# Batch 0's decay rows issued by SP instead of GpSimd, and pair 1's K transposed one tile earlier with half of its copy on ScalarE

## The chip, the cores and the metric

The kernel runs on one core of a Trainium2 chip. The metric is the device time of one execution in microseconds; the time before is the median of three runs. The core's engines are named as in the profile: PE (TensorE), DVE (VectorE), ACT (ScalarE), POOL (GpSimd) and SP (SyncE). SP and POOL also issue the DMAs.

## The reference

Forgetting attention, followed by a small MLP. Shapes: 8 batches, 8 heads, 576 positions, head dimension 64; the MLP takes 4608 tokens of width 512 to 2048 and back.

```python
scores = scale * np.matmul(q, k.transpose(0, 1, 3, 2))
cum = np.cumsum(np.log(np.clip(f, 0.0001, 1.0)), axis=-1)
scores = np.where(causal, -1e9, scores + cum[..., :, None] - cum[..., None, :])
attn = softmax(scores);  x = (attn @ v) laid out as tokens x 512
h = x @ w_in;  out = (h - np.tanh(h)) @ w_out
```

The softmax is a plain one over the last axis. Results are float32.

## The kernel before

**Tiling.** The work of attention goes by pairs of heads: 8 batches x 4 pairs = 32 pairs, called p = 0 to 31 here. For a pair the kernel needs `QT` and `KT`, Q and K turned so that the head dimension lies on the partitions (64 rows), and three more rows under them that carry the decay: the scores' matmul runs over 67 rows, so that `cum[i] - cum[j]` comes out of the same product. The rows are two fp16 parts of the cumulated logarithm (`chi`, `clo`, L189 and L190) and constants (from `ones16` and `minus16`).

`scores` (L337) makes the seven tiles of a pair (`TILES`, L332: three for head 0, a small "tail" tile, index 3, with the last 64 positions of both heads, and three for head 1). In batch 0 the causal mask is added by another matmul with `late` (L355). Each tile ends in an exponential on ACT (L361, target `e`, or `el` for the tail tile). `values` (L382) multiplies by V, DVE divides (L398 to L400), `turn` (L407) puts the result into `XR`, and the MLP (`mlp1` L441, `mlp2_plain` L486, `mlp2` L506) follows in chunks of 512 tokens.

**Transposing Q and K.** `trans` (L287) transposes a pair's Q or K with six matmuls into a PSUM tile `t` (L298) and copies it out in two halves, even and odd positions. The string `copies` says who makes each half: "VV" is twice DVE (L311), "AV" is ACT (L309) for the first and DVE for the second. The two halves interleave in the same rows of `QT` or `KT`.

**Order.** Each engine's order is the order in which the program emits (a manual schedule). `start` (L570) makes pair 0's Q and K and its tiles 0 and 1; `bulk` (L209) issues the rest of batch 0's loads; then `att_items` (L591) lists, for each pair p and tile index `ti`, the scores, the transposes for the next pair (`at_q` and `at_k` say at which tile), the loads of `LOADS`, and `unread(n)` (L563): n matmuls of 128 columns on constants that nobody reads. In pair 0, `unread` stands after tiles 2, 5 and 6. Their PSUM tile `idle` has the bank "tr", which in batch 0 the tail tile of pair 0 and tile 0 of pair 1 use as well (L338, L339). The tiles 4, 5 and 6 use the two banks "sc".

**DMAs.** POOL issues all loads of q, k, v and the weights; they share its software queue (q0 in the profile). A software DMA waits for the one eight places earlier to have ended. SP issues the constant rows (`const_rows`, L202), the decay rows of batch 1 and later (`load_aug`, L198), the DMA transposes and the stores, on its own hardware queue (q1). Before, the three decay rows of batch 0 (seven heads each; head 0 has its rows from ACT at L572 and DVE at L191) go out from POOL at L211 to L213:

```python
(k_hi, chi_0), (k_lo, clo_0), (q_hi, _) = aug_rows(0)
nc.gpsimd.dma_start(out=k_hi, in_=chi_0)
nc.gpsimd.dma_start(out=q_hi, in_=chi_0)
nc.gpsimd.dma_start(out=k_lo, in_=clo_0)
```

The first work that reads these rows is the second head of pair 0's tail tile: head 1 is the first head whose rows come by DMA.

Of the kernel before, what the change touches and what calls it, by code (L numbers as in the profile page):

```python
# [21 lines left out]
def kernel(  # L22
# [10 lines left out]
    nc = tc.nc  # L33
# [7 lines left out]
    NPAIR = H // 2  # L41
# [51 lines left out]
    qn, kn = ([t[0:S // NT6, :].rearrange("p (h n d) -> p h n d", h=H, n=NT6) for t in raw] for raw in (qraw, kraw))  # L93
# [3 lines left out]
    KT = [qkp.tile([D + 3, H, PITCH], FP16, tag=f"KT{i}", name=f"KT{i}") for i in range(2)]  # L97
# [3 lines left out]
    def load_qk(dst, src, b, h0, h1):  # L101
        nc.gpsimd.dma_start(  # L102
            out=dst[b % 2][:, h0:h1, :, :].rearrange("p h n d -> p h (n d)"),
            in_=src[b, h0:h1, :, :].rearrange("h (p n) d -> p h (n d)", n=NT6))
# [25 lines left out]
    def load_v_block(b, n, h0, h1):  # L130
        nc.gpsimd.dma_start(out=vn[b % 2][:, n, h0:h1, 0:D],  # L131
                            in_=v[b, h0:h1, n * P:(n + 1) * P, :].rearrange("h p d -> p h d"))
# [60 lines left out]
    def aug_rows(b):  # L193
        i, h0 = b % 2, 0 if b else 1
        hs = slice(b * H + h0, (b + 1) * H)
        return [(KT[i][D:D + 1, h0:H, 0:S], chi[hs, :]), (KT[i][D + 1:D + 2, h0:H, 0:S], clo[hs, :]), (QT[i][D + 2:D + 3, h0:H, :], chi[hs, :])]

    def load_aug(b):  # L198
        for to, of in aug_rows(b):
            nc.sync.dma_start(out=to, in_=of)  # L200

    def const_rows(i):  # L202
        h0 = 1 - i
        nc.sync.dma_start(out=QT[i][D:D + 2, h0:H, :], in_=minus16[0:2 * (H - h0), :])
        nc.sync.dma_start(out=KT[i][D + 2:D + 3, h0:H, 0:S], in_=ones16[0:H - h0, :])
# [2 lines left out]

    def bulk():  # L209
        (k_hi, chi_0), (k_lo, clo_0), (q_hi, _) = aug_rows(0)  # L210
        nc.gpsimd.dma_start(out=k_hi, in_=chi_0)  # L211
        nc.gpsimd.dma_start(out=q_hi, in_=chi_0)
        nc.gpsimd.dma_start(out=k_lo, in_=clo_0)  # L213
        load_qk(qn, q, 0, 4, 6)
        load_qk(kn, k, 0, 4, 6)
        load_qk(qn, q, 0, 6, H)
        load_qk(kn, k, 0, 6, H)
        for n in range(NJ - 1):
            load_v_block(0, n, 2, H)
# [22 lines left out]
    for b in range(2, B):  # L242
        p0 = (b - 1) * NPAIR
        at_q = [(p0 - 2, n + 2) for n in range(NJ)]
        at_k = [(p0, n) for n in range(NJ)]
# [4 lines left out]
        if b == FAR:  # L250
            at_q = [(p0 - 1, n + 1) for n in range(NJ)]
# [122 lines left out]
    AV = {}  # L374
# [216 lines left out]
    def att_items(p):  # L591
        def put(fn, *args):
            items.append((lambda: fn(*args), True))

        items = []
        here = pairs[p] if p < len(pairs) else None
        before = pairs[p - 1] if 0 < p <= len(pairs) else None
        after = pairs[p + 1] if p + 1 < len(pairs) else None
        early = p < NPAIR
        for ti in range(len(TILES)):  # L600
            if here and (p > 0 or ti > 1):
                put(scores, *here, ti)
            if p == 1 and ti == 6:
                items.append((lambda: const_rows(1), False))
                items.append((lambda: load_aug(1), False))
            if p == 0 and ti in (2, 5, 6):
                put(unread, {2: 6, 5: 4, 6: 6}[ti])
            if p == 1 and ti == 6:
                put(unread, 8, True)
            if p == 1 and ti == 3:  # L610
                put(last)
            for load in LOADS.get((p, ti), ()):
                items.append((load, False))
            at_q, at_k = (1, 3) if p == 0 else (0, 1) if early else (0, 2) if p == NPAIR else (0, 3)
            if p in (2 * NPAIR - 1, 2 * NPAIR, 2 * NPAIR + 1) and (ti % 2 or ti == 0):
                items.append((rest, False))
            if p in (2 * NPAIR - 1, 2 * NPAIR) and ti % 2 == 0:
                pair = pairs[2 * NPAIR + 2 * (p - 2 * NPAIR + 1) + ti // 4]
                put(trans, *pair, *((kn, KT) if ti % 4 else (qn, QT)), False, "VA")
            if ti == at_q and p < 2 * NPAIR - 1:  # L620
                put(trans, *after, qn, QT, early, "VV")
            if p == NPAIR:
                if ti in (4, 5):
                    put(mlp1, 0, ti - 4, 1)
            if ti == at_k and p < 2 * NPAIR - 1 and p != NPAIR:
                put(trans, *after, kn, KT, early, "AV" if early and p > 1 else "VV")
            if p == NPAIR:
                if ti == 1:
                    put(turn, *pairs[p - 2])
                    put(values, *before)  # L630
                    put(mlp1, 0, 0, 0)
                elif ti == 2:
                    put(mlp1, 0, 1, 0)
                    put(turn, *before)
                    put(trans, *after, kn, KT, early, "VV")
            elif early and ti in (2, 4) and before:
                put(values, *before, (ti // 2 - 1,))
            elif not early and ti == 2 and before:
                put(values, *before, (0, 1), p == NPAIR + 2)
            if p < NPAIR:  # L640
                if ti == 1 and p > 1:
                    put(turn, *pairs[p - 2], True)
            elif p > NPAIR and ti == 3:
                items.append((release, False))
                put(turn, *before)
        return items
# [5 lines left out]
    at = 0  # L652
    start()
    bulk()
    for p in range(len(pairs) + 1):
        b, c = divmod(p, NPAIR)
        items = att_items(p)
        take = TAKE[p] if p < len(TAKE) else 8 - (p - len(TAKE)) % 2
        if p == 2 * NPAIR - 1:
            keep()  # L660
        if p == 2 * NPAIR + 1:
            KEPT.clear()
            widen(1)
        mine = mlp[at:at + take]
        at += take
        first = 14 if p == NPAIR else 0
        if p == len(pairs):
            for fn, *args in mine[0:2]:
                fn(*args)
            mine = mine[2:]  # L670
        given, n = 0, 0
        whole = sum(counts for _, counts in items)
        for emit, counts in items:
            emit()
            n += counts
            while n > first and given < len(mine) and given * (whole - first) < (n - first) * len(mine):
                fn, *args = mine[given]
                fn(*args)
                given += 1
# [31 lines left out]
```

## Time and profile before

| what | us |
|---|---|
| runs shown | 533.96, 339.88, 339.72; median 339.88 |
| profiled execution, its time | 340.08 |
| span in the profile | 338.4 |
| PE busy in the span | 331.6 (98%) |
| DVE, ACT, POOL busy | 261.1, 233.5, 162.6 |
| PE's first useful scores (L352) | at 9.12 |
| first MLP matmul (L451) | at 28.71 |

Times inside the trace count from the start of the span. A timeline line gives start, duration, engine, line and operation, and in brackets the idle time ahead of it and what ended it. A line of the chain of waits gives start, length and what the end of the program waited for in that stretch. Matmuls overlap in their pipeline, so the start to start distance is what one costs, not its duration. The granted PE clock is 1.00 in every stretch.

### The profile page before, as it was taken

What the parts mean: (1) busy time and instruction counts of PE and PEld (TensorE: products, weight loads), DVE (VectorE), ACT (ScalarE), POOL (GpSimd) and SP (SyncE); (2) the same over time, 40 slices, a digit from 0 to 9 for tenths busy, and PEclk for the clock granted to TensorE, in tenths of its full rate; (3) what the DMA queues carried; (4) which work ended last, traced back from release to release, by engine and by line L of the source; (5) the groups of instructions that cost most, each with busy time, mean ns of one, the idle gap of its engine ahead of it and who ended that gap; (6) DMA issues with size and microseconds to landing.
All of it is one profiled execution on the core that took longest, in us unless ns stands there. A gap on an engine that the chain in (4) does not pass through costs nothing.

```text
span 338.4 us, 8760 instructions
## 1 busy us (share of the span) xinstructions
PE 331.6 (98%) x3329; PEld 237.4 (70%) x3329; DVE 261.1 (77%) x509; ACT 233.5 (69%) x438; POOL 162.6 (48%) x323
## 2 busy tenths in 40 slices
PE   8899999999999999999999999999999999999995
PEld 8675558875587558855888888656875686486485
DVE  7798986659888887678967796788667866966865
ACT  6798777888977886778677867787558733632630
POOL 8985566775657573677277637632322210000000
PEclk9999999999999999999999999999999999999999
DMA  8999999999969998999799999990130022002003
GB/s 110 130 196 198 186 198 177 182 157 171 138 92 169 143 132 90 135 175 146 96 120 175 132 112 113 166 131 17 50 110 8 17 67 95 2 31 95 0 17 110
DMA packets 147504, 38.82 MB, mean 115 GB/s; under 512 B 128217, under 2 KB 146371, under 8 KB 147462
## 3 DMA queue, kind: packets, MB, share of 16 engines
q0 software_dynamic: 94592, 18.38, 70.8%
q1 hardware_dynamic: 52864, 19.87, 33.2%
q8 instruction: 26, 0.43, 0.5%
q14 instruction: 16, 0.13, 0.2%
q10 hardware_dynamic: 6, 0.01, 0.0%
HBM read 36.85 MB, written 9.44 MB: 137 GB/s over the span
## 4 chain that ended last, share of the span: by engine, by line
PE 91%; DVE 2%; POOL 2%; ACT 2%; DMA 1%; issue 1%; ACTq 0%
PE hps L451 36%; PE ops L517 29%; PE ps L352 12%; PE av L389 8%; PE ops L492 4%; ACT e L361 2%; PE t L298 1%; DMA KT<-clo 1%; DVE KT L311 1%; DVE QT L311 0%; POOL vn L127 0%; POOL qn L102 0%; PE x L417 0%; POOL kn L102 0%; DVE xn L400 0%
## 5 line engine op out<-in xcount | busy, mean ns | idle before, releaser
L451 PE MATMUL hps<-XR,win 128*128 128x512 f16 (+1 forms) x640 | 140.7, 357 | 0.3 <-ACT XR L421 0.2
L456 ACT ACTIVATE th<-hps 128x512 f32<-128x512 f32 x144 | 86.6, 602 | 55.1 <-PE hps L451 53.5
L361 ACT ACTIVATE e<-ps 128x512 f16<-128x512 f32 x192 | 110.4, 598 | 9.6 <-PE ps L352 7.0
L462 DVE TENSOR_TENSOR gq<-hps,th 128x512 f16<-128x512 f32 x144 | 98.1, 687 | 23.5 <-ACT th L456 22.1
L371 POOL TENSOR_SCALAR_AFFINE_SELECT e<-e 128x128 f16<-128x128 f16 x168 | 59.2, 356 | 72.5 <-ACT e L361 70.5
L451 PEld LDWEIGHTS <-win 128*128 128x128 f16 x640 | 57.8, 97 | 48.6 <-issue 0.7
L352 PE MATMUL ps<-QT,KT 67*128 67x64 f16 (+4 forms) x384 | 76.5, 276 | 1.8 <-ACT e L361 0.6
L517 PEld LDWEIGHTS <-gq 128*128 128x128 f16 x640 | 60.3, 97 | 11.1
L517 PE MATMUL ops<-wout,gq 128*128 128x256 f16 x512 | 63.2, 272 | 0.0
L352 PEld LDWEIGHTS <-KT 67*128 67x128 f16 x384 | 36.5, 98 | 22.9 <-issue 1.3
L389 PEld LDWEIGHTS <-e 128*128 128x128 f16 x896 | 32.3, 97 | 3.6
L389 PE MATMUL av<-vn,e 128*128 128x65 f16 x896 | 33.6, 193 | 0.0
L131 POOL DMA_DIRECT2D vn<-in_v_dram x32 | 28.0, 879 | 7.1 <-DMA win<-in_moe_w_in_dram 3.3
L517 PE MATMUL ops<-W,sq 128*128 128x256 f16 x256 | 31.2, 272 | 0.0
L400 DVE TENSOR_TENSOR xn<-av,rs 128x640 f16<-128x640 f32 x32 | 26.4, 825 | 1.3 <-DVE rs L399 0.2
L517 PEld LDWEIGHTS <-sq 128*128 128x128 f16 x256 | 24.1, 98 | 3.4
L371 POOL TENSOR_SCALAR_AFFINE_SELECT el<-el 128x128 f16<-128x128 f16 x28 | 9.3, 332 | 26.8 <-ACT el L361 26.5
L108 POOL DMA_DIRECT2D qn<-in_q_dram x25 | 21.2, 846 | 1.8 <-issue 1.4
L108 POOL DMA_DIRECT2D kn<-in_k_dram x25 | 21.1, 846 | 1.7 <-issue 1.4
L398 DVE TENSOR_SCALAR rs<-av 128x10 f32<-128x10 f32 x32 | 5.2, 162 | 18.1 <-PE av L389 17.0
L311 DVE COPY KT<-t 64x576 f16<-64x576 f16 (+1 forms) x20 | 14.7, 736 | 3.7 <-PE t L298 3.5
L532 ACT ACTIVATE m<-ops 128x512 f32<-128x512 f32 x16 | 9.5, 596 | 10.9 <-PE ops L517 10.9
(85 smaller groups left out, 319.2 us busy)
## 6 DMA issues: line engine op xcount, KB each, us to landing
out_dram<-ost SPq DMA_DIRECT2D x34, 256.0 KB
vn<-in_v_dram POOLq DMA_DIRECT2D x24, 128.0 KB, 6.1
qn<-in_q_dram POOLq DMA_DIRECT2D x20, 128.0 KB, 4.6
kn<-in_k_dram POOLq DMA_DIRECT2D x20, 128.0 KB, 4.9
win<-in_moe_w_in_dram POOLq DMA_DIRECT2D x2, 1024.0 KB, 12.1
wout<-in_moe_w_out_dram POOLq DMA_DIRECT2D x2, 1024.0 KB, 15.7
XR<-xn SPq DMA_TRANSPOSE x56
qn<-in_q_dram POOLq DMA_DIRECT2D x6, 144.0 KB, 4.5
```

What stands on the lines that cost most here:

```text
L108: nc.gpsimd.dma_start(out=dst[b % 2][0:pn, n, :].rearrange("p (h d) -> p h d", h=H), in_=src[b, :, n * P:n * P + pn, :].rearrange("h p d - ...
L131: nc.gpsimd.dma_start(out=vn[b % 2][:, n, h0:h1, 0:D], in_=v[b, h0:h1, n * P:(n + 1) * P, :].rearrange("h p d -> p h d"))
L311: nc.vector.tensor_copy(out=to, in_=of)
L352: nc.tensor.matmul(out=ps[:, col:col + n], lhsT=kt[0:rows, h, j * P:(j + 1) * P], rhs=qt[0:rows, h, i0:i0 + n], start=True, stop=cut == 0)
L361: nc.scalar.activation(out=e[:, lo:hi], in_=ps[:, lo:hi], func=AF.Exp, bias=-SHIFT, scale=qscale)
L371: nc.gpsimd.affine_select(out=view, in_=view, compare_op=ALU.is_ge, fill=0.0, base=0, pattern=pat, channel_multiplier=-1)
L389: nc.tensor.matmul(out=av[:, a, ib, :], lhsT=E.pop((b, c, a, j, ib)), rhs=vn[b % 2][:, j, 2 * c + a, 0:D + 1], start=(j == 0), stop=(j == ib))
L400: nc.vector.tensor_tensor(out=xn.rearrange("p i (a d) -> p a i d", a=2), in0=av[:, :, :, 0:D], in1=rs.to_broadcast([P, 2, NJ, D]), op=ALU. ...
L451: nc.tensor.matmul(out=hps[:, o:o + n], lhsT=win[:, ci, ft * P:(ft + 1) * P], rhs=XR[:, ci, t:t + n], start=(ci == 0), stop=(ci == NCH - 1))
L456: nc.scalar.activation(out=th, in_=hps, func=AF.Tanh, scale=-1.0)
L462: nc.vector.tensor_tensor(out=GQ[(u, i)][:, half, kt, :], in0=hps, in1=th, op=ALU.add)
L517: nc.tensor.matmul(out=ps[:, m, :], lhsT=LHS[lhs](u, kt // 4)[:, kt % 4, m * P:(m + 1) * P], rhs=rhs[:, kt, :], start=(fresh and (apart or ...
```

## The change

The three decay rows of batch 0 are issued by SP instead of POOL. On SP they stand behind batch 0's constant rows and ahead of batch 1's constant rows (which `const_rows(1)` and `load_aug(1)` emit in pair 1). On POOL they stood ahead of batch 0's remaining loads of q, k and v.

In pair 0, K of the next pair is transposed after tile 2 instead of after tile 3, so ahead of the tail tile on PE, and its first half is copied by ACT instead of DVE. ACT's copy stands ahead of the tail tile's exponential. The `unread` after tile 6 grows from 6 matmuls to 10.

```diff
     def bulk():
         (k_hi, chi_0), (k_lo, clo_0), (q_hi, _) = aug_rows(0)
-        nc.gpsimd.dma_start(out=k_hi, in_=chi_0)
-        nc.gpsimd.dma_start(out=q_hi, in_=chi_0)
-        nc.gpsimd.dma_start(out=k_lo, in_=clo_0)
+        nc.sync.dma_start(out=k_hi, in_=chi_0)
+        nc.sync.dma_start(out=q_hi, in_=chi_0)
+        nc.sync.dma_start(out=k_lo, in_=clo_0)
...
             if p == 0 and ti in (2, 5, 6):
-                put(unread, {2: 6, 5: 4, 6: 6}[ti])
+                put(unread, {2: 6, 5: 4, 6: 10}[ti])
...
-            at_q, at_k = (1, 3) if p == 0 else (0, 1) if early else (0, 2) if p == NPAIR else (0, 3)
+            at_q, at_k = (1, 2) if p == 0 else (0, 1) if early else (0, 2) if p == NPAIR else (0, 3)
...
             if ti == at_k and p < 2 * NPAIR - 1 and p != NPAIR:
-                put(trans, *after, kn, KT, early, "AV" if early and p > 1 else "VV")
+                put(trans, *after, kn, KT, early, "AV" if early and p != 1 else "VV")
```

## The prediction

> **What bounds the kernel now.** I read the page's busy times first, then the chain of waits cut to the first 52 us, then the timelines of ACT, POOL, SP and DVE up to 30 us, and last the DMA queues in windows of half a microsecond and less.
>
> ```profile
> PE 331.6 (98%) x3329; PEld 237.4 (70%) x3329; DVE 261.1 (77%) x509; ACT 233.5 (69%) x438; POOL 162.6 (48%) x323
> ```
>
> PE is busy 98% of the span. From the first MLP matmul on (28.71) the only wait of PE in the list is 0.2 us; the rest of the chain there is PE with a few exponentials. The change moves no work of that part, so it can only shift the moment at which that part begins, and such a shift passes to the end one to one. Before that moment PE's "busy" holds fillers that nobody reads, so the chain is needed:
>
> ```profile
> 8.21 3.65 DMA KT<-clo
> ...
> 11.94 0.19 PE ps L352
> 12.13 0.03 PE ps L355
> 12.16 0.26 PE t L298 x6
> ...
> 12.73 0.60 ACT e L361
> 13.34 0.04 issue
> 13.38 0.30 PE ps L352
> ...
> 13.88 0.35 PE idle L566 x6
> 14.23 0.04 issue
> 14.27 0.38 PE ps L352
> ...
> 15.00 0.81 DVE QT L311
> ```
>
> The reader is to see: POOL's third decay row (issued at 8.21) lands at 11.86. PE, at the tail tile since 11.14, starts its second head at 11.94. Then come pair 1's K transposes, tile 4 with its exponential at 12.73, tile 6 at 13.38 (its bank is freed by that exponential), six fillers, and tile 0 of pair 1 at 14.27. Behind it stand pair 2's Q transposes; DVE copies them from 15.00 and then has no gap until 19.59. What the change is worth is the shift of 14.27.
>
> ACT's timeline has its gap at the same place, and shows what a K copy costs there:
>
> ```profile
> 12.20 0.28 ACT L361 ACTIVATE el<-ps 128x128 f16<-128x128 f32 x1 [0.82 <-PE ps L355]
> ...
> 24.04 0.82 ACT L309 ACTIVATE KT<-t 64x576 f16<-64x576 f16 x1
> 24.70 0.60 ACT L361 ACTIVATE e<-ps 128x512 f16<-128x512 f32 x1
> ```
>
> ACT stands idle 0.82 us ahead of the tail's exponential. A K half lasts 0.82 us, but the next exponential starts 0.66 us after it (0.67 at 19.91 to 20.58).
>
> **Part 1: three rows from POOL to SP.** POOL loses three issues, 7.17 to 8.71. Its loads after them start about 1.5 us earlier. I cost this at nothing: the chain names no load after 8.21, and pair 2's Q and K (issued 8.71 and 9.36) keep nobody waiting at 14.54. The cover would go only if the earlier loads delayed the rows (below). The rule that a software DMA waits for the eighth before it gives no new stall either: the first ones concerned wait for loads issued before 6.5.
>
> On SP the rows follow the constant rows. SP's first row of `chi` was issued at 6.90, and that is now batch 0's. Its neighbours stood 0.68 to 0.85 us apart, `clo` is ready at 7.72; so k_hi at 6.90, q_hi at 7.6, k_lo at 8.3. That is as late as POOL's 8.21. Queued behind on SP are batch 1's five issues, each some 2.1 us later, for pairs from 26 us on: their cover is over 10 us.
>
> The question is thus how long SP's row takes to land. This view (the hardware queue, 9.5 to 10.0 us) and its neighbours count the packets:
>
> ```profile
> q0 software_dynamic: 80, 0.01, 33.3%
> q1 hardware_dynamic: 24, 0.01, 12.2%
> ```
>
> Counted in steps of 0.1 us, the queue's last three DMAs (issued 6.90, 7.75, 8.43) are through at about 9.35, 9.75 and 10.2: 2.45, 2.0 and 1.8 us after issue. But there the software queue was thin (33% here, above 110% from 10.5). Under full software load, the rows of batch 2 (issued 26.23 to 27.71) are through some 4.6 to 4.9 us after issue. So k_lo lands between 10.1 and 13.2. I take 2.5 us, so 10.8, since the load around 9 us is nearest to what it meets, with the dip now filled by POOL's earlier loads.
>
> Here a rule of the Trainium skill speaks against the change. The row: POOL's own k_lo took 3.65 us, SP's of the same size and time 1.8. The page "DMA: Bandwidth & Descriptors", section "Issuing engines are not separate DMA queues", says that all issuers share the same 16 DMA engines and that another issuer saves only sequencer time. By it alone the row would take 3.65 us again and the time would be 339.9. The same page's "Queues, rings and completion order" lets each engine take queue rows in turn, packet by packet, which agrees with the 1.8.
>
> **Part 2: K's transposes ahead of the tail, half on ACT.** Six transposes follow six fillers: 10.59 + 0.35 = 10.94. They take 0.26, so the tail's heads start at 11.20 and 11.26. The last transpose ends at 10.94 + 0.42 = 11.36, and ACT, whose exponentials end at 11.38, starts K at 11.40. The tail's exponential follows at 11.40 + 0.67 = 12.07, if the row has landed by 12.07 - 0.26 - 0.08 = 11.73 (11.94 to 12.20, and 11.86 to 11.94, before). Tile 4's exponential follows 0.27 later (21.11 to 21.38), at 12.34; before it was 12.73. Bounds: if ACT overlaps nothing (0.82 and 0.28), 12.50.
>
> DVE's half carries a wait for ACT's, as they write interleaved columns (in the trace DVE's KT at 24.97 follows ACT's end at 24.86): 12.22 + 0.03 + 0.81 = 13.06 instead of 14.08. Behind it on DVE is only pair 2's Q near 14.9. Nothing waits.
>
> What is late next: the four fillers after tile 5 use the tail's bank and wait for its exponential. PE is through tile 5 near 11.9 and stands until 12.39. The stall on the DMA becomes one on ACT, about as long.
>
> **Part 3: ten fillers.** Tile 6 comes 0.65 after tile 4's exponential starts (12.73 to 13.38): 12.99. Fillers from 12.99 + 0.50 = 13.49. Six cost 0.35, ten 0.58, so 14.07, and 0.04 later tile 0 of pair 1: 14.11. K is ready by then. The four more cost 0.23 us of what the earlier exponential gives; bounds 0 to 0.4 (0.1 us each is the cold pace, 47 in 4.9 us).
>
> **Sum.** Tile 4's exponential -0.39, fillers +0.23: -0.16 us. The profiled execution took 340.08 (span 338.4 and 1.68 around it), so 339.92. It stands 0.20 above the median of the runs shown (339.88); against that, 339.7.
>
> **The rivals.**
> - *Late row.* The decay row becomes the wait again: POOL's loads, 1.5 us earlier, fill the DMA engines just when SP's rows pass. For it: 4.6 to 4.9 us at 26 us. Against it: 1.8 to 2.45 at 7 to 10 us. Each us after 11.73 costs a us; from 11.89 on the kernel is slower than before. At 13.2 it is -0.16 + 1.47 = +1.3, so 341.2. This one ends on the other side.
> - *Hidden anyway.* ACT pays K in full: tile 4's exponential at 12.50, tile 0 of pair 1 at 14.27, as before; 339.9. The same time comes out if the row takes its old 3.65 us (11.95, +0.06). For it: the gap on ACT that is filled and the copy are both 0.82. Against it: the overlap seen twice.
> - *More.* The additional fillers cost nothing, as some other wait covers them: -0.39, so 339.5. Against it: PE's order has nothing between them and the tile, and they share its bank.
>
> **How the numbers follow.** The forecast (339.7, its own range 339.5 to 339.9): 0.5. Hidden anyway, or the old landing (339.9): 0.2. Late row (340.0 to 341.2): 0.2. More (339.3 to 339.5): 0.1. The range 339.3 to 340.7 leaves out the late half of the late row and something below, under 2 in 10; single runs shown differ by 0.16. A change of 2%, about what a measurement of this kernel can tell from no change, is 6.8 us; no case here reaches it. Faster by over 2%: 0.01; within: 0.97; slower: 0.02, for something unseen.
>
> **What would show it.** In the changed kernel's profile: PE's wait on KT<-clo gone; ACT's KT copy at 11.4, the tail's exponential at 12.1 and tile 4's at 12.3; a wait of PE of about 0.5 us on ACT ahead of the fillers at 12.4; tile 0 of pair 1 near 14.1 and DVE's QT near 14.8; the same intervals as before from there. It is wrong if the wait on the row stays past 11.73, if ACT's copy is the end of the chain at 14.27, or if the distance from 15.00 to the first MLP matmul changes.

## The result and the profile after

The changed kernel takes 340.64 us (median of 18 runs) against 339.88 before: ratio 1.0031, interval 1.0016 to 1.0046. That is 0.2 to 0.3% slower (0.2% between the medians; the ratio has three runs of 342 to 343.5 in it, of which more below): within the 2% that counts as no change, but clear of the noise. The forecast was 339.7; the rival that ended on the other side, the late row, is what happened.

The chain of waits of the changed kernel, cut to the first 52 us (start, length, what the end waited for), answers to the one shown of before:

```profile
8.39 4.03 DMA KT<-clo
12.42 0.34 issue
12.76 0.19 PE ps L352
...
13.02 0.28 ACT el L361
13.30 0.60 ACT e L361
13.90 0.04 issue
13.94 0.30 PE ps L352
...
14.44 0.57 PE idle L566 x10
15.01 0.04 issue
15.05 0.38 PE ps L352
...
15.79 0.81 DVE QT L311
```

The reader is to see: the decay row is still what everything hangs on, and it comes later. Issued by SP at 8.39 it holds PE until 12.76; issued by POOL at 8.21 it held PE until 11.94. Of these 0.82 us, 0.18 are the later issue, 0.38 the longer way to landing (4.03 against 3.65), and 0.26 pass between landing and PE's start (0.34 against 0.08); for the last the trace names no cause. K's transposes no longer stand between the tail and tile 4, but tile 4's exponential starts at 13.30 instead of 12.73, and tile 0 of pair 1 at 15.05 instead of 14.27: +0.78 us. From there nothing is lost or won: the last DVE operation of the chain starts at 334.98 before and 335.77 after, +0.79.

ACT's timeline after shows that the copy went into the gap as planned, and that a gap as large stays behind it:

```profile
11.38 0.80 ACT L309 ACTIVATE KT<-t 64x576 f16<-64x576 f16 x1
13.02 0.28 ACT L361 ACTIVATE el<-ps 128x128 f16<-128x128 f32 x1 [0.83 <-PE ps L355]
```

The issues were as forecast: SP's rows first, then POOL's first load, which before started at 8.71.

```profile
6.90 0.69 SPq L211 DMA_DIRECT2D KT<-chi  x1
7.64 0.71 SPq L212 DMA_DIRECT2D QT<-chi  x1
8.39 0.70 SPq L213 DMA_DIRECT2D KT<-clo  x1
```

```profile
6.99 0.65 POOL L102 DMA_DIRECT2D qn<-in_q_dram  x1
```

So most of the difference lies between issue and landing. The DMA queues between 9.6 and 10.0 us (packets, MB, time as a share of 16 engines; q0 is POOL's software queue, q1 is SP's), first of before, then of after:

```profile
q0 software_dynamic: 44, 0.01, 25.1%
q1 hardware_dynamic: 19, 0.01, 12.5%
```

```profile
q0 software_dynamic: 115, 0.07, 121.8%
q1 hardware_dynamic: 1, 0.00, 0.3%
```

Before, POOL's three tiny issues had left a hole in its queue, and SP's packets (then batch 1's rows, which nobody was waiting for) ran through it. After, POOL's loads close the hole, and in the same 0.4 us one packet of SP's queue gets through. Counted in windows of 0.1 us, the three rows' 42 packets are through at 11.95, the last row 3.6 us after its issue.

### The profile page after: what moved, and what is told of

Read it like the earlier page. It is cut to its first block, busy times and chain, and to the rows that moved or that the text cites. A ratio compares the mean times of both kernels' runs of the same rounds, so it can differ in the third digit from the quotient of the medians.

```text
span 339.0 us, 8766 instructions
## 1 busy us (share of the span) xinstructions
PE 331.5 (98%) x3333; PEld 237.2 (70%) x3333; DVE 260.0 (77%) x508; ACT 234.3 (69%) x439; POOL 161.9 (48%) x320
## 4 chain that ended last, share of the span: by engine, by line
PE 91%; DVE 4%; ACT 2%; DMA 1%; issue 1%; ACTq 0%
PE hps L451 36%; PE ops L517 29%; PE ps L352 12%; PE av L389 8%; PE ops L492 4%; ACT e L361 2%; PE t L298 1%; DMA KT<-clo 1%; DVE KT L311 1%; DVE QT L311 0%; DVE TQ L187 0%; PE x L417 0%; DVE xn L400 0%; DVE clo L190 0%; DVE gq L462 0%
## 5 line engine op out<-in xcount | busy, mean ns | idle before, releaser
L371 POOL TENSOR_SCALAR_AFFINE_SELECT e<-e 128x128 f16<-128x128 f16 x168 | 60.1, 360 | 74.5 <-ACT e L361 71.8
L311 DVE COPY QT<-t 64x576 f16<-64x576 f16 x18 | 14.4, 802 | 4.9 <-PE t L298 4.8
## 6 DMA issues: line engine op xcount, KB each, us to landing
win<-in_moe_w_in_dram POOLq DMA_DIRECT2D x2, 1024.0 KB, 11.2
```

The costliest lines, as they stand in the source:

```text
L311: nc.vector.tensor_copy(out=to, in_=of)
L371: nc.gpsimd.affine_select(out=view, in_=view, compare_op=ALU.is_ge, fill=0.0, base=0, pattern=pat, channel_multiplier=-1)
```

## The experiments

Two theories stood against each other at first. *Late row*: the row on SP is late because the software queue has no hole any more. *Copy and fillers*: ACT's K copy and the ten fillers cost the time. A third was that SP's queue needs its 4 us whatever POOL does. In the table, "second head" is when PE starts the tail's second head (the first use of the rows), "tile 4" its exponential on ACT, "tile 0" tile 0 of pair 1 on PE; these come from each kernel's one profiled execution, the median from all its runs, and the ratio from runs of the kernel before on the same chip.

| kernel | median us | ratio, interval | second head | tile 4 | tile 0 |
|---|---|---|---|---|---|
| before | 339.88 | | 11.94 | 12.73 | 14.27 |
| changed | 340.64 | 1.0031, 1.0016 to 1.0046 | 12.76 | 13.30 | 15.05 |
| e1 rows on POOL | 340.07 | 1.0011, 1.0002 to 1.0019 | 11.67 | 12.20 | 13.96 |
| e2 rows alone on SP | 341.72 | 1.0050, 1.0029 to 1.0072 | 12.74 | 14.06 | 16.32 |
| e3 pause on POOL | 340.00 | 1.0003, 0.9995 to 1.0012 | 11.39 | 12.23 | 13.98 |
| e4 six fillers | 340.30 | 1.0016, 1.0007 to 1.0024 | 12.42 | 12.95 | 14.49 |
| e5 rows on POOL, six fillers | 339.66 | 0.9983, 0.9960 to 1.0005 | 11.49 | 12.20 | 13.72 |
| e6 filled pause, six fillers | 339.59 | 0.9972, 0.9950 to 0.9993 | 11.54 | 12.38 | 13.91 |
| e7 half pause | 339.82 | 0.9981, 0.9961 to 1.0001 | 11.68 | 12.22 | 13.98 |
| e8 e2 with the gap filled | 340.63 | 1.0008, 0.9988 to 1.0029 | 12.69 | 13.48 | 15.02 |
| e9 rows on SP, filled pause alone | 339.50 | 0.9983, 0.9974 to 0.9992 | 11.57 | 12.36 | 13.89 |
| e10 changed, again | 340.70 | 1.0021, 1.0008 to 1.0033 | 12.54 | 13.07 | 14.83 |
| e11 e6, again | 339.57 | 0.9979, 0.9958 to 1.0000 | 11.58 | 12.43 | 13.95 |
| e12 e9 with short memsets | 339.36 | 0.9971, 0.9944 to 0.9997 | 11.37 | 12.16 | 13.70 |

**e1, the rows back on POOL, all else as changed.**

```diff
-        nc.sync.dma_start(out=k_hi, in_=chi_0)     # and q_hi, k_lo
+        nc.gpsimd.dma_start(out=k_hi, in_=chi_0)   # and q_hi, k_lo
```

> The changed kernel with the three decay rows back on POOL; K's earlier transposes, ACT's half copy and the ten fillers stay. Theory 'late row' (the changed kernel is slow because k_lo, issued by SP at 8.39, lets PE go on only at 12.76): k_lo lands at 11.86 again, PE starts the tail's second head at 11.94, tile 4's exponential at 12.47, tile 0 of pair 1 near 14.25, time as before, 339.9. Rival 'the K copy on ACT and the fillers cost the time': tile 0 of pair 1 stays near 15.0 and the time near 340.6.

Measured: PE's start on the second head, first in the changed kernel, then in e1:

```profile
12.76 0.19 PE L352 MATMUL ps<-QT,KT 67*128 67x64 f16 x1 [1.35 <-DMA KT<-clo]
```

```profile
11.67 0.19 PE L352 MATMUL ps<-QT,KT 67*128 67x64 f16 x1 [0.26 <-DMA KT<-clo]
```

PE waits 0.26 us instead of 1.35, tile 4's exponential starts at 12.20, tile 0 at 13.96. So in the trace the copy and the fillers don't cost the 0.78 at tile 0; the rows on SP do. The medians say so for most of it: 340.07 lies 0.57 below the changed kernel, but still 0.2 above where late row put it, and the interval of e1's ratio lies just above 1. The profiled run took 339.80; the runs reach from 339.79 to 340.85.

**e2, the rows alone moved to SP, in the kernel before.**

> The kernel before with only the three rows moved to SP. Theory 'late row': PE's second tail head starts at 12.76 instead of 11.94, and everything behind it by as much later: tile 4's exponential 13.55, K's copies on DVE 13.3 to 14.9, tile 0 of pair 1 near 15.1, 340.7. Rival 'the K copy on ACT and the fillers cost the time': tile 0 of pair 1 near 14.3, 339.9.

Measured: the second head at 12.74, as the theory has it, but tile 0 at 16.32 instead of 15.1. Six of the 12 runs took 340.3 to 340.7, as expected, and six 342.8 to 344.3. The profiled one is of the latter, and its row of stretches (PE, PEld, DVE, ACT, POOL busy; then the granted clock) shows the difference:

```profile
9.00:12.00 3.00, 2.15 (x25) 1.55 (x25) 2.62 (x5) 2.00 (x4) 3.00 (x5) 1.00 1.20 165
12.00:15.00 3.00, 2.25 (x18) 1.71 (x19) 1.46 (x2) 1.22 (x3) 3.00 (x6) 0.53 2.03 152
15.00:18.00 3.00, 2.94 (x24) 2.22 (x23) 0.61 (x2) 1.39 (x3) 2.90 (x5) 0.50 1.43 170
18.00:21.00 3.00, 3.00 (x41) 2.59 (x39) 2.74 (x4) 1.72 (x4) 2.94 (x7) 0.50 1.17 207
21.00:24.00 3.00, 3.00 (x43) 2.44 (x41) 1.55 (x4) 2.05 (x5) 1.81 (x3) 0.76 1.12 207
```

A mean of 0.53 over 12 to 15 us is a clock of 0.50 for 2.8 of the 3 us, so from about 12.2: PE had then stood idle for 0.8 us, and the wait had over 0.5 us to go. By the mean of 0.76 over 21 to 24 us the clock is back at about 22.4. The other five of the six have mean clocks of 0.989 and 0.990 against 0.985 in this one; that is 0.50 for some 7 us, if the clock went to 0.50 there too. Neither theory had this; e8 tests it.

**e3, a pause on POOL in the changed kernel.**

```diff
         nc.sync.dma_start(out=k_lo, in_=clo_0)
+        for _ in range(6):
+            nc.gpsimd.memset(EL[2], 0.0)
```

> The changed kernel with a pause on POOL of the length that the three issues took: six memsets of a tile of 128x192 (0.26 us each) ahead of the loads that follow. Theory 'late row, because the software queue is no longer interrupted': the dip of the DMA engines near 9.5 us is back, k_lo on SP lands 1.8 to 2.5 us after its issue at 8.39, so by 10.9, PE doesn't wait for it, tile 4's exponential starts at 12.34, tile 0 of pair 1 near 14.1, time 339.7. Rival 'SP's rows take some 4 us whatever POOL does': PE's second tail head stays at 12.76 and the time at 340.6.

Measured: POOL's loads start at 8.84 instead of 6.99, PE's second head at 11.39, tile 0 at 13.98. The queues at 9.6 to 10.0 us in this kernel:

```profile
q0 software_dynamic: 17, 0.00, 8.2%
q1 hardware_dynamic: 14, 0.01, 7.3%
```

Those 14 packets are the last row: it is through 1.5 us after its issue at 8.39. Same queue, same issue, and 2 us between them; so it is not SP's queue that is slow. The median fell from 340.64 to 340.00, less than the trace of its own run (339.75); its runs spread from 339.56 to 340.34.

**e4, six fillers instead of ten in the changed kernel** (`6: 10` to `6: 6`).

> The changed kernel with 6 instead of 10 fillers after tile 6 of pair 0. If the four more cost 0.23 us as forecast: tile 0 of pair 1 at 14.82 instead of 15.05 and the time near 340.4. If something else covers them: 15.05 and 340.6.

Measured: from the second head to tile 0 it is 2.07 us instead of 2.29: the four fillers cost 0.22, nothing covers them. That tile 0 came at 14.49 and not 14.82 is the row, which let PE go on 0.34 us earlier in this execution.

**e5, e1 with six fillers.**

> K's earlier transposes and ACT's half copy alone: rows on POOL, six fillers. If the gain of that part is real and the four more fillers take it back (they cost 0.22 us between the first two runs of the changed kernel's order): tile 0 of pair 1 at 13.73, 0.54 earlier than in the profile of the kernel before, time 339.5 to 339.6. Rival, that the typical run of this order waits longer for POOL's row than the profiled one (the median of the run with ten fillers lay 0.27 above its profiled time): 339.8 to 339.9.

Measured: tile 0 at 13.72, time 339.66, ratio 0.9983 with an interval that holds 1: K's move without the SP rows may gain a little, and these runs don't prove it.

**e6, the pause filled with work.** POOL's four memsets for batch 1 (`last`, before in pair 1) move ahead of the loads; rows on SP, six fillers.

```diff
         nc.sync.dma_start(out=k_lo, in_=clo_0)
+        last()
...
-            if p == 1 and ti == 3:
-                put(last)
```

> Rows on SP, six fillers, and the pause on POOL filled with work that it has to do anyway: the four memsets that the kernel does in pair 1 (1.6 us) stand ahead of the loads after the rows. Theory 'the rows need the pause': the row lands before 11.7, PE doesn't wait for it beyond 0.2 us, tile 0 of pair 1 at 13.75, time 339.4 to 339.6, the fastest so far. If the pause was not the reason, 340.4.

Measured: 339.59, and all 12 runs within 339.55 to 339.62, where the kernel before spreads over 0.9 us and more. In its trace PE doesn't wait for the row. Whether that is why the spread is gone stays open: e3 and e12 below have no such wait in their traces either, and spread over 0.78 and 0.44 us. It is faster than before (ratio 0.9972, interval below 1).

**e7, half the pause** (`range(6)` to `range(3)` in e3).

> The changed kernel with half the pause on POOL (three memsets, 0.8 us). If the rows wait for the software queue's packets, k_lo comes between the two: PE's second tail head between 11.4 (full pause) and 12.76 (none), near 12.0; time near 340.2. If only the full pause opens a dip: 12.7 and 340.6; if any pause is enough: 11.4 and 340.0.

Measured: second head at 11.68, close to the full pause (11.39) and 1.1 us from none; time 339.82. The second head hides how far the row moved, as PE reaches the tail's first head only at 11.2 and starts the second about 0.2 later even where it waits for nothing. The packets of SP's queue, counted as above, show a row that comes later the earlier POOL's loads start (e9 is told below):

| kernel | POOL's first load at | last row's packets through, us after its issue | second head |
|---|---|---|---|
| changed, no pause | 6.99 | 3.6 | 12.76 |
| e7, three memsets | 7.81 | 2.7 | 11.68 |
| e9, four memsets of pair 1 | 8.52 | 2.4 | 11.57 |
| e3, six memsets | 8.84 | 1.5 | 11.39 |

So half the pause gives about half of what the row can gain, as the first of the three theories has it, and PE needs no more than that.

**e8, e2 with PE's gap filled** (`2: 6` to `2: 26` fillers after tile 2).

> The kernel before with the rows on SP (as run before) and 26 instead of 6 fillers ahead of the tail tile, which fill 1.2 of the 1.4 us in which PE stood idle for the row; the row and all else as it was. Without the fillers 6 of 12 runs took 342.8 to 344.3 at a mean granted clock of 0.99, and the profiled one showed a clock of 0.5 from 12.7 to about 22 us. Theory 'the idle gap lets the clock fall': no run above 341 now, all near 340.5. Rival 'those runs are slow for a reason of their own (the rows' DMA, chance of the run)': about half still at 343.

Measured: all 12 runs lie within 340.50 to 341.17, one of them just above the 341. The fillers fill the whole gap. The tail's two heads:

```profile
12.47 0.19 PE L352 MATMUL ps<-QT,KT 67*128 67x64 f16 x1
...
12.69 0.19 PE L352 MATMUL ps<-QT,KT 67*128 67x64 f16 x1
```

The second follows the first by 0.22 us and without a wait, as it does where the row is early (11.35 and 11.57 in e9), so 12.69 does not tell when the row landed. The queues do: from 9.6 to 10.0 us POOL's queue is at 132.8% and no packet of SP's gets through, and the last row's packets are through at about 12.0 (12.2 in e2). So the row was about as late as in e2. The clock of the profiled run:

```profile
12.00:15.00 3.00, 2.73 (x37) 2.06 (x35) 1.70 (x3) 1.70 (x4) 3.00 (x6) 1.00 1.96 163
15.00:18.00 3.00, 2.98 (x60) 2.51 (x60) 2.22 (x3) 2.77 (x6) 2.50 (x5) 1.00 1.67 182
```

So the clock falls because PE stands idle, in some runs, and fillers in the gap prevent it; the late row alone doesn't do it. How long a gap must be is not shown: in e2 the clock fell 0.8 us into it. In e2 the late row has two prices: 0.6 us in every run, and some 2.5 us more (3.8 in the profiled one) in half of them.

**e9, rows on SP and the filled pause, without K's move** (e2 with e6's edit).

> The kernel before with the rows on SP and the pause on POOL filled with the four memsets of pair 1; K's transposes where they were, both copies on DVE, six fillers. Theory 'the row's landing is all that counts, and K's move to ACT is worth something only while the row is late': the row is there by 11.4, K's transposes follow at 11.6, DVE copies K from 12.0 to 13.7, tile 0 of pair 1 near 13.8, and the time is that of the run with the filled pause and the moved K, 339.6, give or take 0.15. Rival 'K's earlier transposes and ACT's half are worth 0.4 us by themselves', as the first sum had it: 340.0.

**e10 and e11, the changed kernel and e6 again, beside e9 on one chip.**

> The changed kernel as it is, on the same chip and beside the others of this call, for a second look at where its rows land: k_lo keeps PE until 12.4 to 12.8 again, 340.6; some runs above 341.5 with a mean clock below 0.997.

> The run with rows on SP, filled pause, moved K and six fillers again, beside the changed kernel: 339.6, all runs within 0.1 of one another, since nothing waits for the row any more.

Measured: 339.50 (e9), 340.70 (e10), 339.57 (e11). One run of e10 took 342.67 at a mean clock of 0.995. The runs of e11 reach from 339.50 to 339.75, more than the 0.1 expected. Once the row is early, K's move is worth nothing: e9 without it has tile 0 at 13.89, e11 with it at 13.95. ACT's lines, of e9 and of e11, show why:

```profile
11.83 0.28 ACT L362 ACTIVATE el<-ps 128x128 f16<-128x128 f32 x1 [0.23 <-PE ps L356]
12.36 1.09 ACT L362 ACTIVATE e<-ps 128x512 f16<-128x512 f32 x2 [0.26 <-PE ps L356]
```

```profile
11.60 0.81 ACT L310 ACTIVATE KT<-t 64x576 f16<-64x576 f16 x1
12.28 0.25 ACT L362 ACTIVATE el<-ps 128x128 f16<-128x128 f32 x1
12.43 1.07 ACT L362 ACTIVATE e<-ps 128x512 f16<-128x512 f32 x2
```

The gap that the copy was to fill was itself made by the late row. Without it the copy stands in front of the tail's exponential and delays it from 11.83 to 12.28; what PE saves, ACT pays.

**e12, e9 with the pause made of e3's six short memsets.**

> As the run with the rows on SP and the pause alone, but the pause made of six short memsets (128x192) that the kernel doesn't need, instead of the four of pair 1. In the runs with those four, DVE's copy at L191 took 0.49 us instead of 0.30 while POOL's memset of 64x528 ran, and PE's first scores came at 9.3 instead of 9.12. If that memset is the reason: L191 0.30 again, first scores at 9.12, tile 0 of pair 1 near 13.7 and 339.3. If moving POOL's work has nothing to do with it: 9.3, 13.9 and 339.5.

Measured: tile 0 at 13.70 and 339.36, the fastest median of all, ratio 0.9971 (0.9944 to 0.9997). DVE's copy at L191, of e9 (beside POOL's memset of 64x528, 7.56 to 8.09) and of e12:

```profile
7.77 0.49 DVE L191 COPY KT<-clo 3x576 f16<-3x576 f16 x1
```

```profile
7.76 0.30 DVE L191 COPY KT<-clo 3x576 f16<-3x576 f16 x1
```

The 0.19 us pass to the first scores (9.33 against 9.13) and to tile 0 (13.89 against 13.70).

## Why the prediction was wrong, point by point

- **Where the change acts, and that it passes one to one: right.** A shift of 0.78 at tile 0 is 0.79 at the end and 0.76 in the medians.
- **Part 1, the landing of the row: the step that failed.** "I take 2.5 us, so 10.8." Measured: issue at 8.39 (forecast 8.3), packets through at 11.95, landing by the chain at 12.42, PE's start at 12.76. With the 0.08 us that the prediction allowed between landing and PE's start, that is a landing at 12.68, 1.9 us late. About 1.1 of the 1.9 are the packets, 3.6 us instead of 2.5. The 2.5, 2.0 and 1.8 us were read in the hole that POOL's three issues made in the software queue, and the change removes exactly these. The prediction named the hole as filled and still took a value measured in it. The row under full load (4.6 to 4.9 us) was as far off on the other side; the range of 10.1 to 13.2 held what was measured. Another 0.5 us pass between the last packet and the landing (11.95 to 12.42), which a count of packets leaves out, and 0.3 more than allowed between landing and PE's start; why is open. The table at e7 shows the dependence on POOL's loads: 3.6 us without a pause, 1.5 with the longest.
- **"I cost this at nothing" (POOL's earlier loads): wrong.** Nobody waits for the loads, as said; but the earlier loads delay the row. The early loads are the cost of the change, not its gain.
- **The late row rival: right, given 0.2.** Its formula has -0.16 + (12.68 - 11.73) = +0.79; measured +0.78. What this tests is the way from the second head to tile 0, since 12.68 is worked back from PE's start: 2.30 us by the formula, 2.29 measured.
- **Part 2, K's move: the times were about right where the row is early, the gain was put down to the wrong thing.** Tile 4's exponential was forecast at 12.34, and starts at 12.20 to 12.23 in e1 and e3, 0.14 us after the tail's instead of 0.27. But e12 has it at 12.16 without K's move (e9 at 12.36, its first scores 0.2 late): the -0.39 was the row, not the copy. On the late path K's move takes 0.26 us of transposes off the way and the fillers put 0.22 back: from second head to tile 0 it is 2.33 us before and 2.29 after.
- **DVE's half after ACT's (12.22) and part 3 (0.23, measured 0.22): right.**
- **Left out: the clock.** No step priced PE standing idle for 1.4 us. In the changed kernel 4 of 29 runs took 342.0 to 343.5 at a mean clock below 0.997; the median hardly shows it. The kernel before, whose wait is 0.58 us in its profile, has such runs too: 7 of the 114 beside the experiments, none of 35 in one set and 3 of 17 in another, so how much more often the changed kernel has them stays open. The nine kernels whose traces have PE waiting 0.3 us or less for the row (e1, e3, e5 to e9, e11, e12) have none in 104 runs.

On the Trainium skill's rule that the prediction weighed ("DMA: Bandwidth & Descriptors", "Issuing engines are not separate DMA queues"): another issuer saves only sequencer time. The trace agrees with it without the pause (3.65 us from POOL, 4.03 from SP, both to landing by the chain), and it would have put the time nearer than the sum did. The same page's "Queues, rings and completion order" has an engine take the queues in turn, whole packets of several descriptors at a time. No run here tests that: from 9.5 to 11.0 us 15 packets of SP's queue go through beside 354 of POOL's after the change, so those that the profile counts do not alternate one for one, and it doesn't say how many of them make one packet of the page. The skill's "TensorE: Matmul & The Clock Gate" (Part 1) has the clock halve after an idle window of about 3.4 us: the half agrees with the 0.50 of e2, the length does not, since there the clock fell 0.8 us into an idle gap of 1.4 us.

Open: the medians of e1 and e3 lie 0.25 us above their profiled runs. For e1 a landing of POOL's row that varies would do it; for e3, where the row is early in the trace, it would not, and no run here tells.

## What to carry to other kernels

A latency read from the trace belongs to the load that stood beside it; if the change moves that load too, read it where the load is as it will be, and read it to the moment at which the waiting engine starts, not to the last packet. A pause on one issuing engine can be what lets another queue's small, urgent transfer through: put the urgent one first and fill the pause with work that must be done anyway. Before work is moved into an idle gap, ask what makes the gap: here it went away with its cause, and the moved work then stood in the way.

## What the runs showed of the hardware

- A DMA of seven rows of 1152 bytes from SP's hardware queue took 1.5 us until its packets were through when POOL's software queue was at 8% of the engines' time (e3, 9.6 to 10.0 us), and 3.6 us when it was at 122% (changed kernel, the same stretch). In the changed kernel PE started another 0.8 us after the last packet.
- In the profiled run of e2 PE's granted clock fell to 0.50 at about 12.2 us, 0.8 us into an idle gap of 1.4 us, and stayed there for some 10 us. 6 of the 12 runs of e2 had a mean clock of 0.985 to 0.990 and took 342.8 us or more, and none of 12 when 20 more matmuls that nobody reads filled the gap (e8).
- A DVE copy of 3x576 took 0.49 us instead of 0.30 beside a POOL memset of 64x528 (e6, e9, e11), and 0.30 beside memsets of 128x192 (e12). Why the one and not the other was not tried.
